# Newton chain of the later blocks in steps 12 to 23 of a fused attention and rational feed-forward kernel

## The chip, the cores and the metric

The kernel runs on one core of a Trainium2 chip. The metric is the device time of one launch in microseconds. A core has five engines with queues of their own, each of which runs its instructions in the order in which they were written: TensorE (PE: matrix products; PEld: its weight loads), VectorE (DVE), ScalarE (ACT), GpSimd (POOL) and SyncE (SP, which issues nearly all transfers here). TensorE writes to the accumulation memory PSUM; VectorE and ScalarE reach both memories, GpSimd only SBUF.

## The reference

Attention inside chunks of 64 positions, then a feed-forward layer with a rational function between its two products:

```python
scores = scale * np.matmul(q_c, k_c.transpose(0, 1, 2, 4, 3))
attn = np.exp(scores - np.max(scores, axis=-1, keepdims=True))
attn = attn / (np.sum(attn, axis=-1, keepdims=True) + 1e-09)
x = np.matmul(attn, v_c)          # then rearranged to 4608 tokens x 512
h = x @ w_in                      # 512 x 2048
P = a[0] + a[1] * h + a[2] * h**2 + a[3] * h**3
Q = 1.0 + np.abs(b[0]) * np.abs(h) + np.abs(b[1]) * h**2
out = (P / (Q + 1e-6)) @ w_out    # 2048 x 512
```

All is float32. Each operand of the large products is split into a high part in TensorE's rounded format and a low part, and three of the four products of parts are summed.

## The kernel before

The tokens are cut into 18 blocks of 256, and the 2048 hidden columns into four stages, so that there are 72 steps. For blocks 0 and 1 the stages alternate; from step 8 on step g is stage g mod 4 of block g div 4. The order of all instructions is written out by hand.

A step has a first product `ff1` (F and f, 48 matrix instructions) into a PSUM tile `ph` of four 128 x 256 pieces; a chain of elementwise instructions, which turns `ph` into g = P/Q split into `ghi` and `glo`; and a second product `ff2` (Z, z and y, 48 instructions, Z and z with `ghi`, y with `glo`) into `po`, two steps later (`LAG`). There are two `ph` buffers, for even and odd steps, and two each of the SBUF tiles A, B, C, `ghi` and `glo`.

Three stretches follow one another:

- The first stage, the string `START`, loads and splits the weights and runs steps 0 to 11 up to their chains.
- The loop over g from `FIRST` = 12 to `CHANGE` = 24, blocks 3 to 5, with the old chain. On ScalarE: Abs and Square of `ph` into A and B, a2 + a3 h into C (a, b, c; lines 351, 355, 359), Ln of Q (line 367) and Exp of its negative (line 371). On VectorE: Q (line 363), the two Horner steps of P (lines 375, 379), `ghi` = P/Q (line 384), and two instructions for the rounding remainder (lines 388, 392). On GpSimd: `glo` (line 397). Around the chain stand the attention of the next blocks: maximum and scale of the scores (M, U), Exp (E, in blocks 4 to 7 sixteen small instructions), sum and scaling (n, N) in stage 0, transposes and their copy (T, K) behind stage 1, the product with V into `psx`, whose tile is the `ph` buffer of the next step, and its split (X on ScalarE, Y on VectorE) in stage 2, together with the scores `pss` of the block after.
- The string `STEADY`, blocks 6 to 17, with the Newton chain (lines 449 to 489): U = |h|, C = na2 + na3 h, V = (U + c0) U, Ln of V, Exp of its negative written over `ph`, two Horner steps of P (p, p2), and t, A2, g, which refine the reciprocal once and multiply. In these blocks the second product uses sums of weights and sums of parts of g (`fast`).

The sums of weights that the later blocks need are made in the loop on GpSimd, one set of four per stage of the second weight: `sums_of` yields groups of instructions, parted by None. In a step with (g - 12) mod 3 of 0 or 1, `make_sums` issues four additions (lines 554 to 566) ahead of the step; in the third, two copies to `hh` on ScalarE (lines 582, 583) and four subtractions in place in `tt` on GpSimd (line 570) are issued, and SP stores `hh` and `tt` in DRAM (lines 574, 575). There is one `tt`, so that the next set begins when its transfer has been read. `newton_coefficients`, called behind step 20, fills the small tile `co`.

```python
for g in range(FIRST, CHANGE):
    ...
    if (g - FIRST) % 3 < 2:
        make_sums()
    one("F f a b", g)
```

Of the kernel before, what the change touches and what calls it, by code (L numbers as in the profile page):

```python
# [10 lines left out]
F32 = mybir.dt.float32  # L11
F32R = mybir.dt.float32r
I32 = mybir.dt.int32
AF = mybir.ActivationFunctionType
ALU = mybir.AluOpType
# [3 lines left out]
P = 128  # L19
# [10 lines left out]
LAG = 2  # L30
KLN = 32
# [16 lines left out]
)  # L48
FIRST = 12
FAST = 6  # L50
CHANGE = NST * FAST
# [14 lines left out]
def tile_chunked_attention_rational_moe(  # L66
# [11 lines left out]
    nc = tc.nc  # L78
    cp = ctx.enter_context(tc.tile_pool(name="cp", bufs=1))
    p2 = ctx.enter_context(tc.tile_pool(name="p2", bufs=2))  # L80
# [13 lines left out]
    ab = cp.tile([P, 8], F32, tag="ab", name="ab")  # L94
    cst = cp.tile([P, 2], F32, tag="cst", name="cst")
    a0, a1, a2, a3 = (ab[:, i:i + 1] for i in range(4))
    b0, b1a = ab[:, 4:5], ab[:, 6:7]
    CQ = 1.0 + 1e-6
    WS = 256.0

    TINY = 2.0 ** -60
# [23 lines left out]
    def load_v(n):  # L125
        if n >= NB:
            return
        v = p2.tile([P, W], F32, tag="vt", name=f"v{n}", bufs=1)
        nc.sync.dma_start(out=v, in_=vP[n])
        loaded["v", n] = v  # L130
# [176 lines left out]
    def att_av(n, u=None, tag="pa"):  # L307
        psx = have("x", n, lambda: bank_pair(tag, f"psx{n}"))

        def cols(g):  # L310
            v, hp = divmod(g, NHP)
            return slice(hp * 128 + v * 64, hp * 128 + v * 64 + 64)

        quarters(cols, psx, loaded["v", n], att["at", n], u)
# [110 lines left out]
                )  # L425
        before[0] = "ff2"

    def newton_coefficients(co):
        na0, na1, na2, na3, c0, kq, lsc, ebias, ib, b1m, nib = (co[:, i:i + 1] for i in range(11))
        ts = nc.vector.tensor_scalar  # L430
        ts(b1m, b1a, TINY, None, ALU.max)
        nc.vector.reciprocal(ib, b1m)
        nc.scalar.activation(ebias, b1m, AF.Ln)
        nc.scalar.activation(c0, b0, AF.Abs, scale=ib)
        ts(nib, ib, -1.0, None, ALU.mult)
        ts(kq, ib, CQ, None, ALU.mult)
        ts(lsc, b1m, 2.0 ** -KLN, None, ALU.mult)
        ts(co[:, 0:4], ab[:, 0:4], nib, None, ALU.mult)
        ts(ebias, ebias, -KLN * math.log(2.0), None, ALU.add)

    total = NB * NST

# [109 lines left out]
    def sums_of(s, tt, hh):  # L552
        def whole(dst, k, half):
            nc.gpsimd.tensor_add(dst, w_part(0, k, s, half).bitcast(F32), w_part(1, k, s, half).bitcast(F32))

        T = [tt[:, i] for i in range(4)]
        yield None
        yield lambda: whole(T[1], 0, 0)
        yield lambda: whole(T[3], 0, 1)
        yield lambda: nc.gpsimd.tensor_sub(T[1], T[3], T[1])  # L560
        yield lambda: whole(T[2], 1, 1)
        yield None
        yield lambda: nc.gpsimd.tensor_add(T[3], T[2], T[3])
        yield lambda: nc.gpsimd.tensor_add(T[2], T[2], T[1])
        yield lambda: whole(T[0], 1, 0)
        yield lambda: nc.gpsimd.tensor_sub(T[0], T[0], T[2])
        yield None

        def low(i):
            nc.gpsimd.tensor_sub(tt[:, i], tt[:, i], hh[:, i].bitcast(F32))  # L570

        def send():
            scratch[s] = dr.tile([P, 2, 4, 512], F32, tag=f"t{s}", name=f"t{s}")
            nc.sync.dma_start(out=scratch[s][:, 0], in_=hh.bitcast(F32))
            nc.sync.dma_start(out=scratch[s][:, 1], in_=tt)
            if s >= 2:
                scratch["b", s] = dr.tile([P, 2, 2, 256], F32, tag=f"b{s}", name=f"b{s}")
                rows = slice(FPS * s, FPS * s + 3, 2)
                for h in range(2):
                    nc.sync.dma_start(out=scratch["b", s][:, h], in_=wo.bitcast(F32)[:, h, rows, 256:512])  # L580

        yield lambda: nc.scalar.copy(hh[:, 1:4:2], tt[:, 1:4:2])
        yield lambda: nc.scalar.copy(hh[:, 0:3:2], tt[:, 0:3:2])
        for i in (1, 3, 2):
            yield lambda i=i: low(i)
        yield lambda: (low(0), send())
# [148 lines left out]
    def ph_tag(g):  # L735
        return "p1" if g == 1 or (g >= 10 and g % 2 == 0) else "p0"
# [18 lines left out]
    def qk(n, u=None):  # L755
# [4 lines left out]

    of_step = lambda f: lambda g: f(*steps[g])
    do = {
        "k": consts, "B": coefficients, "q": qk, "v": load_v, "w": w_load,
        "o": w_low, "s": w_scale, "j": w_join, "i": w_sign, "e": w_sign_dve, "h": w_hi, "hd": w_hi_dve,
        "d": lambda j: w_diff(nc.vector, j), "dp": lambda j: w_diff(nc.gpsimd, j), "r": w_rest, "l": w_lo,
        "S": att_s, "M": att_max, "U": att_sub, "E": att_exp, "n": att_rs, "N": att_norm,
# [14 lines left out]
    def run(program, then=""):  # L781
        words_ = [re.fullmatch(r"([A-Za-z]+)([0-9.]+)(?::(\w+))?", item).groups() for item in program.split()]
        letters = [name for name, _, _ in words_] + [then]
        for k, (name, args, tag) in enumerate(words_):
            ahead[0] = next((x for x in letters[k + 1:] if x in ("F", "f", "Z", "z", "y", "r")), "")
            do[name](*map(int, args.split(".")), **({"tag": tag} if tag else {}))
# [1 line left out]
    run(START, "F")  # L788


    co = p2.tile([P, 32], F32, tag="co", name="co", bufs=1)
    na0, na1, na2, na3, c0, kq, lsc, ebias, ib, b1m, nib = (co[:, i:i + 1] for i in range(11))
    tt = p2.tile([P, 4, 512], F32, tag="raw", name="tt", bufs=3)
    hh = p2.tile([P, 4, 512], F32R, tag="raw", name="hh", bufs=3)
    qk = p2.tile([P, 2, W], F32, tag="raw", name="qk", bufs=3)
    making = [f for s in range(NST) for f in sums_of(s, tt, hh)][1:]

    chain = {
        "U": new_u, "C": new_c, "V": new_v, "p": new_p, "p2": new_p2, "Ln": new_ln, "Ex": new_exp, "t": new_t,
        "A2": new_inv, "g": new_g, "hR": new_hr, "lR": new_lr, "s1": new_s1, "s2": new_s2, "s4": new_s4,  # L800
        "hS": new_hs, "lS": new_ls,
    }
# [84 lines left out]
    def make_sums():  # L887
        while making:
            f = making.pop(0)
            if f is None:  # L890
                break
            f()
# [4 lines left out]
            nc.sync.dma_start(out=qk[:, i, :], in_=src[n])  # L897

    one = lambda names, k: run(" ".join(f"{x}{k}" for x in names.split()))
    for g in range(FIRST, CHANGE):  # L900
        n, stage = steps[g]
        m, early = n + 1, n + 2
        if (g - FIRST) % 3 < 2:
            make_sums()
        one("F f a b", g)
        if stage == 0:
            one("n N", m)
        one("c Q", g)
        if stage == 3:
            one("M U", early)  # L910
        if stage == 2:
            att_av(m, tag=ph_tag(g + 1))
            load_v(m + 1)
            one("S", early)
            load_scores(early + 1)
            one("X", m)
        one("I p", g)
        if stage == 2:
            one("Y", m)
        one("J P", g)  # L920
        if stage == 3:
            one("E", early)
        sums = making[:6] if (g - FIRST) % 3 == 2 else []
        for f in sums[:2]:
            f()
        one("g H R Gp", g)
        for f in sums[2:]:
            f()
        del making[:len(sums) and 7]
        if g == CHANGE - 4:  # L930
            newton_coefficients(co)
        back = steps[g - LAG]
        run(" ".join(f"{x}{g - LAG}" for x in "Zzy"), "F")
        fetch_behind(*back)
        if back[1] == NST - 1:
            store(back[0])
        if stage == 1:
            one("T K", m)

    items = [re.fullmatch(r"(\w+?)(?:_(\d))?([+-]\d+)?", item).groups() for item in STEADY.split()]  # L940
    for b in range(FAST, NB + 1):
        order = list(items)
        if b == NB - 1:
            tail_load()
            order.remove(("hR", "2", None))
            order.insert(order.index(("C", "3", None)) + 1, ("hR", "2", None))
        for op, stage, shift in order:
            n = b + int(shift or 0)
            if n >= NB:
                continue  # L950
            if stage is not None:
                g = NST * n + int(stage)
                if g >= (CHANGE - LAG if op[0] == "Z" else CHANGE):
                    step_op(op, g)
            elif op in ("P1", "o1", "o2", "o3", "o4"):
                if NB - 1 > n >= FAST:
                    fast_out(n, ("P1", "o1", "o2", "o3", "o4").index(op))
                elif op == "P1" and n == FAST - 1:
                    store(n)
            elif n > FAST + (op in ("S", "M", "U", "E")):  # L960
                attention[op](n)
# [36 lines left out]
```

## Time and profile before

| | us |
|---|---|
| median of three runs | 890.44 |
| lowest and highest | 886.53, 891.39 |
| the profiled execution | 888.72 |
| its span, first to last instruction | 886.9 |
| TensorE busy in the span | 847.7 |
| VectorE, ScalarE, GpSimd busy | 770.1, 567.6, 532.4 |
| mean granted TensorE clock | 0.992 |

The profile is one execution, taken by the hardware profiler. Busy times count each engine's instructions; an engine's idle time has a releaser, the instruction that the next one waited for. The granted clock is given as a share of TensorE's full speed. Lines named L384 and so on are those of the kernel before.

### The profile page before, as it was taken

To read this page: it belongs to the slowest core of one execution; us is meant where nothing else is said; L and a number is where in the kernel's file an instruction comes from. 1 tells how busy PE (TensorE), PEld (TensorE's weight loads), DVE (VectorE), ACT (ScalarE), POOL (GpSimd) and SP (SyncE) were. 2 spreads that over 40 slices of the span, in tenths; PEclk is the share of its full clock that TensorE was granted. 3 is DMA by queue.
4 is the path that set the end of the run, shared out by engine and by line. 5 is a ranking of instruction groups with operands and counts; after the bars stand their busy time and mean duration, and the time that the engine had idled before them with its cause. 6 is when DMAs were issued, how large, how long until landed. Compare 5 with 4: busy or idle time off the path is not lost.

```text
span 886.9 us, 21207 instructions
## 1 busy us (share of the span) xinstructions
PE 847.7 (96%) x9108; PEld 831.8 (94%) x9108; DVE 770.1 (87%) x662; ACT 567.6 (64%) x693; POOL 532.4 (60%) x320
## 2 busy tenths in 40 slices
PE   2799999998989899999999999999999999999997
PEld 1689999998989899999999999999999999999996
DVE  6799999879899987888888898889888988887785
ACT  4799986556765556666666666666666666666552
POOL 0114310146687787777868686868686767776771
PEclk9799999999999999999999999999999999999999
DMA  7544250303114155576768677777777777775861
GB/s 290 185 167 167 96 190 14 109 2 126 66 50 143 60 180 175 186 248 198 242 218 256 217 248 229 239 236 237 238 238 232 238 232 238 226 232 172 283 209 36
DMA packets 125469, 162.85 MB, mean 184 GB/s; under 512 B 6848, under 2 KB 111296, under 8 KB 122304
## 3 DMA queue, kind: packets, MB, share of 16 engines
q1 hardware_dynamic: 125216, 161.25, 55.7%
q8 instruction: 71, 1.16, 0.5%
q10 hardware_dynamic: 160, 0.26, 0.1%
q14 instruction: 22, 0.18, 0.1%
HBM read 142.61 MB, written 18.87 MB: 182 GB/s over the span
## 4 chain that ended last, share of the span: by engine, by line
PE 80%; DVE 9%; ACT 5%; DMA 4%; issue 2%; POOL 0%; DVEq 0%; ACTq 0%
PE ph L347 39%; PE acc L606 14%; PE acd L606 11%; PE po L423 10%; PE psx L219 2%; DMA raw<-in_w_in 2%; DMA wo<-t 2%; PE pss L219 2%; DVE B L363 2%; PE pst L299 2%; DVE ghi L384 1%; DVE B L388 1%; DVE C L379 1%; DVE C L375 1%; PE pl L198 1%
## 5 line engine op out<-in xcount | busy, mean ns | idle before, releaser
L347 PE MATMUL ph<-xhi,wi_hi 128*128 128x256 f32 x1152 | 322.4, 280 | 3.2 <-DVE xlo L330 1.6
L347 PE MATMUL ph<-xlo,wi_hi 128*128 128x256 f32 x1152 | 321.1, 279 | 0.1
L347 PE MATMUL ph<-xhi,wi_lo 128*128 128x256 f32 x1152 | 320.9, 279 | 0.0
L347 PEld LDWEIGHTS ph<-xhi,wi_hi 128*128 128x128 f32 x1152 | 218.4, 190 | 4.7 <-DVE xlo L330 1.8
L347 PEld LDWEIGHTS ph<-xlo,wi_hi 128*128 128x128 f32 x1152 | 217.5, 189 | 0.5 <-DVE xlo L330 0.4
L347 PEld LDWEIGHTS ph<-xhi,wi_lo 128*128 128x128 f32 x1152 | 217.5, 189 | 0.0
L541 POOL TENSOR_TENSOR slo<-B,shi 128x1024 fp32r<-128x1024 f32 x46 | 110.7, 2406 | 69.1 <-ACT shi L533 66.9
L451 ACT ACTIVATE U<-ph 128x1024 f32<-128x1024 f32 x48 | 49.5, 1031 | 142.4 <-PE ph L347 142.4
L397 POOL TENSOR_TENSOR glo<-B,A 128x1024 fp32r<-128x1024 f32 x16 | 49.0, 3065 | 97.7 <-DVE B L392 64.4
L460 DVE SCALAR_TENSOR_TENSOR U<-U,co 128x1024 f32<-128x1024 f32 x48 | 84.2, 1754 | 21.7 <-ACT U L451 21.0
L517 POOL TENSOR_TENSOR B<-C 128x512 f32<-128x512 f32 x46 | 69.7, 1515 | 54.6 <-DVE C L489 49.1
L423 PE MATMUL po<-wo,ghi 128*128 128x256 f32 (+2 forms) x768 | 93.6, 278 | 0.0
L481 DVE SCALAR_TENSOR_TENSOR U<-U,co,ph 128x1024 f32<-128x1024 f32 x48 | 60.5, 1259 | 37.6 <-ACT ph L477 37.6
L423 PEld LDWEIGHTS po<-wo,ghi 128*128 128x128 f32 x768 | 90.2, 188 | 0.3
L509 POOL TENSOR_TENSOR graw<-C,graw 128x768 fp32r<-128x768 f32 x46 | 85.4, 1857 | 0.7 <-ACT graw L504 0.7
L606 PE MATMUL acc<-wo,graw 128*128 128x256 f32 x552 | 79.5, 279 | 0.0
L606 PEld LDWEIGHTS acc<-wo,graw 128*128 128x128 f32 x552 | 70.1, 188 | 0.7
L473 ACT ACTIVATE B<-U,cst,co 128x1024 f32<-128x1024 f32 x48 | 59.8, 1246 | 16.4 <-DVE U L460 16.1
L522 POOL TENSOR_TENSOR B<-C,B 128x256 f32<-128x256 f32 x46 | 64.5, 1402 | 3.6
L489 DVE SCALAR_TENSOR_TENSOR C<-C,co,ph 128x1024 f32<-128x1024 f32 x48 | 61.5, 1281 | 1.7
L468 DVE SCALAR_TENSOR_TENSOR C<-C,co,ph 128x1024 f32<-128x1024 f32 x48 | 61.4, 1278 | 1.3
L477 ACT ACTIVATE ph<-B,co 128x1024 f32<-128x1024 f32 x48 | 53.8, 1121 | 12.4 <-DVE C L468 12.4
(118 smaller groups left out, 1850.0 us busy)
## 6 DMA issues: line engine op xcount, KB each, us to landing
wo<-t SPq DMA_DIRECT2D x90, 768.0 KB, 6.6
wo<-t SPq DMA_DIRECT2D x98, 256.0 KB, 3.4
out<-o SPq DMA_DIRECT2D x68, 128.0 KB, 6.2
raw<-in_w_in SPq DMA_DIRECT2D x8, 1024.0 KB, 4.9
raw<-in_w_out SPq DMA_DIRECT2D x8, 1024.0 KB, 5.0
v<-in_vP SPq DMA_DIRECT2D x20, 256.0 KB, 7.8
qk<-in_qT SPq DMA_DIRECT2D x36, 128.0 KB, 6.8
qk<-in_kT SPq DMA_DIRECT2D x36, 128.0 KB, 6.4
```

The costliest lines, as they stand in the source:

```text
L347: nc.tensor.matmul(ph[:, fi, :], w[:, cc, f], x[:, cc, :], start=(k == 0), stop=(k == len(mm) - 1))
L423: nc.tensor.matmul(accs[n][i][:, cols], g[:, fi, i * 128:(i + 1) * 128], w[:, FPS * s + fi, cols], start=start, stop=stop,)
L460: nc.vector.scalar_tensor_tensor(U, U, c0, U, ALU.add, ALU.mult)
L468: nc.vector.scalar_tensor_tensor(C, C, na1, h, ALU.add, ALU.mult)
L473: nc.scalar.activation(ch[key][2], ch[key][1], AF.Ln, bias=cst[:, 0:1], scale=lsc)
L481: nc.vector.scalar_tensor_tensor(V, V, kq, h, ALU.add, ALU.mult)
L489: nc.vector.scalar_tensor_tensor(C, C, na0, h, ALU.add, ALU.mult)
L509: nc.gpsimd.tensor_sub(lo, quads(ch[steps[g]][3])[:, :, 1:4, :], hi.bitcast(F32))
L517: nc.gpsimd.tensor_sub(S[:, 0:2], q[:, 0:1].to_broadcast([P, 2, 2, 128]), q[:, 1:3])
L522: nc.gpsimd.tensor_sub(S[:, 2], q[:, :, 1, :], S[:, 1])
L541: nc.gpsimd.tensor_sub(lo, sbuf[g], hi.bitcast(F32))
L606: nc.tensor.matmul(acc[n][pair][:, bank, col:col + 256], stat, mov, start=start, stop=stop)
```

## The change

Steps 12 to 23 take the Newton chain that the later blocks have. In step g the copy to `ghi` and the subtraction for `glo` are those of step g - 1 (`hR`, `lS`), and for step 23 they follow in `STEADY`. The tile `co` is made ahead of `START`, and the coefficients are computed in `START`: maximum and reciprocal on VectorE (D0) behind block 4's maximum, seven small instructions on ScalarE (C0) ahead of block 4's Exp. The copies to `hh`, the subtractions and the stores of a set of sums stand at the end of their step, behind the second product, the block's store and the transposes' copy, and not between the chain's instructions.

```diff
-    "v4 Z9 c10 Gp9 A3:p0 p10 X3 I10 J10 P10 I11 Y3 S4:pa g10 J11 g11 H10 R10 H11 M4 R11 U4 y8 Gp11 G10 E4 y9 "
+    "v4 Z9 c10 Gp9 A3:p0 p10 X3 I10 J10 P10 I11 Y3 S4:pa g10 J11 g11 H10 R10 H11 M4 D0 R11 U4 y8 Gp11 G10 C0 E4 y9 "
...
+    def newton_reciprocal(_):
+        nc.vector.tensor_scalar(b1m, b1a, TINY, None, ALU.max)
         nc.vector.reciprocal(ib, b1m)
-        nc.scalar.activation(ebias, b1m, AF.Ln)
-        nc.scalar.activation(c0, b0, AF.Abs, scale=ib)
-        ts(nib, ib, -1.0, None, ALU.mult)
-        ts(kq, ib, CQ, None, ALU.mult)
-        ts(lsc, b1m, 2.0 ** -KLN, None, ALU.mult)
-        ts(co[:, 0:4], ab[:, 0:4], nib, None, ALU.mult)
-        ts(ebias, ebias, -KLN * math.log(2.0), None, ALU.add)
+
+    def newton_coefficients(_):
+        act = nc.scalar.activation
+        act(c0, b0, AF.Abs, scale=ib)
+        act(nib, ib, AF.Copy, scale=-1.0)
+        act(kq, ib, AF.Copy, scale=CQ)
+        act(lsc, b1m, AF.Copy, scale=2.0 ** -KLN)
+        act(co[:, 0:4], ab[:, 0:4], AF.Copy, scale=nib)
+        act(ebias, b1m, AF.Ln)
+        act(ebias, ebias, AF.Identity, bias=cst[:, 1:2])
...
-        one("F f a b", g)
+        one("F f", g)
+        chain_ops("U C", g)
         if stage == 0:
             one("n N", m)
-        one("c Q", g)
+        if g > FIRST:
+            chain_ops("hR lS", g - 1)
+        chain_ops("V", g)
         if stage == 3:
             one("M U", early)
...
-        one("I p", g)
+        chain_ops("Ln p", g)
         if stage == 2:
             one("Y", m)
-        one("J P", g)
+        chain_ops("p2 Ex", g)
         if stage == 3:
             one("E", early)
-        sums = making[:6] if (g - FIRST) % 3 == 2 else []
-        for f in sums[:2]:
-            f()
-        one("g H R Gp", g)
-        for f in sums[2:]:
-            f()
-        del making[:len(sums) and 7]
-        if g == CHANGE - 4:
-            newton_coefficients(co)
+        chain_ops("t A2 g", g)
         back = steps[g - LAG]
...
         if stage == 1:
             one("T K", m)
+        if (g - FIRST) % 3 == 2:
+            make_sums()
...
-                if g >= (CHANGE - LAG if op[0] == "Z" else CHANGE):
+                if g >= (CHANGE - LAG if op[0] == "Z" else CHANGE - 1 if op == "hR" else CHANGE):
```

## Rows read from the trace of the kernel before

**Rows 1.** The page's first part: busy us, share of the span, instructions.

```profile
PE 847.7 (96%) x9108; PEld 831.8 (94%) x9108; DVE 770.1 (87%) x662; ACT 567.6 (64%) x693; POOL 532.4 (60%) x320
```

**Rows 2.** Windows: stretch, length, busy us by engine, granted clock, DMA share, GB/s.

```profile
186.00:345.00 159.00, 149.48 (x1620) 148.29 (x1620) 142.69 (x104) 104.18 (x211) 117.96 (x61) 0.99 0.26 94
...
309.30:313.00 3.70, 3.38 (x128) 3.35 (x128) 3.63 (x4) 3.70 (x5) 0.00 (x0) 0.54 0.86 332
```

**Rows 3.** Timeline of TensorE: start, duration, instruction, idle time before it.

```profile
199.73 1.04 PE L299 MATMUL pst<-ident,e 128*128 128x128 f32 x8
200.53 0.37 PE L347 MATMUL ph<-xhi,wi_hi 128*128 128x256 f32 x1
...
208.16 0.45 PE L219 MATMUL psx<-at,v 64*64 64x64 f32 x14 [1.94 <-ACT at L303]
...
210.19 0.40 PE L423 MATMUL po<-wo,ghi 128*128 128x280 f32 x1
217.53 0.39 PE L347 MATMUL ph<-xhi,wi_hi 128*128 128x256 f32 x1 [1.61 <-DVE xlo L330]
...
259.15 0.46 PE L219 MATMUL psx<-at,v 64*64 64x64 f32 x16 [2.26 <-ACT at L303]
...
309.62 0.49 PE L219 MATMUL psx<-at,v 64*64 64x64 f32 x7 [3.60 <-ACT at L303]
...
318.81 0.29 PE L347 MATMUL ph<-xhi,wi_hi 128*128 128x256 f32 x1
```

**Rows 4.** Groups by line, the old chain: busy us, mean ns, idle before.

```profile
L397 POOL TENSOR_TENSOR glo<-B,A 128x1024 fp32r<-128x1024 f32 x16 | 49.0, 3065 | 97.7 <-DVE B L392 64.4 <-DVE sm L263 17.3 <-PE ph L347 7.9
...
L384 DVE SCALAR_TENSOR_TENSOR ghi<-C,ab,A 128x1024 fp32r<-128x1024 f32 x24 | 40.5, 1688 | 1.9 <-ACT A L371 0.3
...
L388 DVE SCALAR_TENSOR_TENSOR B<-B,ghi 128x1024 f32<-128x1024 f32 x24 | 36.4, 1517 | 0.5
```

**Rows 5.** The same groups, of the Newton chain in the later blocks.

```profile
L541 POOL TENSOR_TENSOR slo<-B,shi 128x1024 fp32r<-128x1024 f32 x46 | 110.7, 2406 | 69.1 <-ACT shi L533 66.9 <-DMA wo<-t 1.3
...
L460 DVE SCALAR_TENSOR_TENSOR U<-U,co 128x1024 f32<-128x1024 f32 x48 | 84.2, 1754 | 21.7 <-ACT U L451 21.0
...
L489 DVE SCALAR_TENSOR_TENSOR C<-C,co,ph 128x1024 f32<-128x1024 f32 x48 | 61.5, 1281 | 1.7
...
L464 DVE TENSOR_TENSOR C<-C,ph 128x1024 f32<-128x1024 f32 x48 | 58.1, 1211 | 0.1
...
L477 ACT ACTIVATE ph<-B,co 128x1024 f32<-128x1024 f32 x48 | 53.8, 1121 | 12.4 <-DVE C L468 12.4
...
L499 ACT CAST ghi<-C 128x1024 fp32r<-128x1024 f32 x2 | 2.1, 1044 | 4.0 <-DVE C L489 4.0
```

**Rows 6.** Timelines of VectorE (scaling of block 4; coefficients) and the chain's Exp.

```profile
191.96 2.08 DVE L290 TENSOR_TENSOR e<-e,sm 128x1024 f32<-128x1024 f32 x1
...
300.97 2.10 DVE L438 TENSOR_SCALAR co<-ab,co 128x4 f32<-128x4 f32 x1
...
186.06 4.85 ACT e L274 x32
```

**Rows 7.** Timeline of GpSimd, sums of weights.

```profile
225.21 6.04 POOL L570 TENSOR_TENSOR tt<-tt,hh 128x512 f32<-128x512 f32 x4
237.50 3.99 POOL L554 TENSOR_TENSOR tt<-wo 128x512 f32<-128x512 f32 x2 [6.25 <-DMA t<-tt]
...
265.02 7.01 POOL L570 TENSOR_TENSOR tt<-tt,hh 128x512 f32<-128x512 f32 x4
276.48 2.56 POOL L554 TENSOR_TENSOR tt<-wo 128x512 f32<-128x512 f32 x2 [4.45 <-DMA t<-tt]
...
313.31 2.96 POOL L554 TENSOR_TENSOR tt<-wo 128x512 f32<-128x512 f32 x2 [4.32 <-DMA t<-tt]
```

**Rows 8.** The chain that ended last: start, us, a second and a first product.

```profile
324.45 5.44 PE po L423 x48
329.89 5.48 PE ph L347 x48
```

More of the change, by code (lines that the diff above doesn't have):

```diff
@@ L426, in ff2 @@
         before[0] = "ff2"
[L428 to L431, printed above, removed]
+    co = p2.tile([P, 32], F32, tag="co", name="co", bufs=1)
+    na0, na1, na2, na3, c0, kq, lsc, ebias, ib, b1m, nib = (co[:, i:i + 1] for i in range(11))
+    def newton_reciprocal(_):
+        nc.vector.tensor_scalar(b1m, b1a, TINY, None, ALU.max)
         nc.vector.reciprocal(ib, b1m)
-        nc.scalar.activation(ebias, b1m, AF.Ln)
-        nc.scalar.activation(c0, b0, AF.Abs, scale=ib)
-        ts(nib, ib, -1.0, None, ALU.mult)
-        ts(kq, ib, CQ, None, ALU.mult)
-        ts(lsc, b1m, 2.0 ** -KLN, None, ALU.mult)
-        ts(co[:, 0:4], ab[:, 0:4], nib, None, ALU.mult)
-        ts(ebias, ebias, -KLN * math.log(2.0), None, ALU.add)
+    def newton_coefficients(_):
[7 more added lines that the diff above has]
+        act(ebias, ebias, AF.Identity, bias=cst[:, 1:2])
     total = NB * NST
@@ L762, in tile_chunked_attention_rational_moe @@
     do = {
-        "k": consts, "B": coefficients, "q": qk, "v": load_v, "w": w_load,
+        "k": consts, "B": coefficients, "C": newton_coefficients, "D": newton_reciprocal, "q": qk, "v": load_v, "w": w_load,
         "o": w_low, "s": w_scale, "j": w_join, "i": w_sign, "e": w_sign_dve, "h": w_hi, "hd": w_hi_dve,
@@ L788, in tile_chunked_attention_rational_moe @@
     run(START, "F")
-    co = p2.tile([P, 32], F32, tag="co", name="co", bufs=1)
-    na0, na1, na2, na3, c0, kq, lsc, ebias, ib, b1m, nib = (co[:, i:i + 1] for i in range(11))
     tt = p2.tile([P, 4, 512], F32, tag="raw", name="tt", bufs=3)
@@ L899, in tile_chunked_attention_rational_moe, with chain_ops @@
     one = lambda names, k: run(" ".join(f"{x}{k}" for x in names.split()))
+    def chain_ops(names, g):
+        for name in names.split():
+            chain[name](g)
     for g in range(FIRST, CHANGE):
```

## The prediction

> **What bounds the kernel now.** Read first the busy line of the page [rows 1]: TensorE has 847.7 us of the 886.9 us span, so time is lost only where its queue stops. Steps 12 to 23 lie between about 186 and 345 us; over that window TensorE is busy 149.48 of 159.00 us, VectorE 142.69 and GpSimd 117.96 [rows 2]. The TensorE rows with idle time before them name the stops: 1.94 us before psx in step 14, 1.61 before the first product of step 15, 2.26 before psx in step 18, 3.60 before psx in step 22 [rows 3]: 9.4 us, against 9.52 from the window. Behind the 3.60 us stop the clock drops: 0.54 granted over 3.70 us [rows 2], between the 1.2 and the 2.4 GHz level, which is 0.46 x 3.70 = 1.7 us of lost work. So 9.5 + 1.7 = 11.2 us is all that a change of these steps can give back.
>
> **The change, by engine load.** Both chains have five ScalarE and six VectorE instructions a step and one on GpSimd. Four of the old VectorE instructions read two SBUF tiles and average 1.52 to 1.69 us; in the new chain only V does (1.75), and the five others read PSUM and take 1.21 to 1.28 [rows 4, 5]. With 1.21 and 1.28 for its two PSUM ones the old six make about 8.8 us, the new six 8.0: 0.8 a step. GpSimd's instruction goes from 3.07 to 2.41 us [rows 4, 5]. The coefficients leave step 20, where seven small VectorE instructions, one of them 2.10 us, stood in front of step 21's chain [rows 6]: at least 2.1 us of VectorE. In the first stage they cost two short VectorE instructions ahead of block 4's scales and seven on ScalarE ahead of its 4.85 us row of Exp at 186.06, which waits for those scales [rows 6]. I let that row slip 0.35 us, two short instructions' worth (bounds 0 and 1.0, the second if ScalarE's seven lie on the path too).
>
> Those 2-SBUF instructions and GpSimd exclude each other in the trace: GpSimd's four subtractions take 6.04 us in step 14 and 7.01 in step 17, and V averages 1.75 us where the same operation with a PSUM operand takes 1.28 [rows 5, 7]. The Trainium skill says the same ("SBUF — State Buffer", Who interferes with whom): a VectorE instruction with two SBUF inputs contends with a GpSimd one that reads SBUF, one with at most one SBUF input does not. By that rule alone, three of four collisions would go and the kernel would get the whole 11.2 us; that is the first rival below. I don't follow it, because queue order decides here.
>
> **What the new order makes later.** (1) The old chain frees the ph buffer after its third VectorE instruction, the new one after its sixth, and that sixth lies behind a round trip to ScalarE (Exp waits for p2, t waits for Exp). Steps in a row cost V 1.2 + p 1.25 + p2 1.2 + Exp 1.15 + t 1.3 + A2 1.25 + g 1.3 = 8.65 us on an idle machine. (2) ghi and glo of step g are made in step g+1: the copy hR behind U and C, the subtraction lS on GpSimd behind the four sum instructions that stand at the head of that step's program. C of step g+2 takes the buffer that lS frees. (3) The copies hh, and with them the low parts and their transfer, come at the step's end, on ScalarE behind store and transposes' copy, on GpSimd behind lS of the step before.
>
> **The walk,** with those prices, 1.3 us for a sum instruction, 1.5 for a low one, 2.4 for lS, 5.48 for a first and 5.45 for a second product [rows 5 to 8], 1.1 more for a collision.
> Step 12: block 4's scaling ends on VectorE at 194.0 [rows 6]; V waits out a sum instruction, ready 196.4; p, p2 198.8; Exp 199.95; t, A2, g 203.9. The first product of step 14 needs that buffer and was due at 200.53 [rows 3]: **a new stop of 3.4 us**. Step 13: V 205.1, p2 207.5, Exp 208.7, g 212.6. psx takes ph of step 13 and would be due at 203.9 + 5.48 = 209.4: **stop of 3.2 us**, in place of 1.94. The second product begins at 212.6 + 2.0 for psx and pss (208.16 to 210.19 [rows 3]) = 214.7 and covers xlo (216.1), so step 15's first product starts at 220.1, not 217.53 [rows 3]: 2.6 us late.
> Steps 15 to 18: four first products, three second ones and 0.8 us of transposes later, at 259.15, psx of step 18 is due; its copy is ready at 256.9 and g of step 17 at 258.9, so there is no stop. The old psx started at 259.15 as well [rows 3]: even. The 2.26 us stop is what pays for the early ones.
> Step 17's sums: hh behind the copy, from 256.8; lows 257.9 to 265.0 (four and a collision); step 18's sum instructions wait for tt to land. The trace has 6.25, 4.45 and 4.32 us of waiting for that [rows 7]; I take 4.4 and keep 6.2 for the range. So 269.4, four instructions and a collision 275.7, lS of step 17 278.1. The last part of its second product is due at 259.15 + 2.0 + 5.45 + 5.48 + 3.63 = 275.7: **stop of 2.4 us**.
> C of step 19 waits for the same lS: 278.2, ready 279.4; p, p2 281.9; Exp 283.1; the block's row of Exp, some 4.7, holds ScalarE to 287.8; scaling and V of step 20 290.8; p2 293.2; Exp 294.4; hh 295.4; lows to 302.5; tt 307.0; sums 313.2; lS of step 20 315.6. TensorE, from 278.2: 1.8, then first and second products with transposes to 308.1, psx and pss 310.1, due 313.7: **stop of 1.9 us**. C of step 22, held by that lS, 316.8; hR 317.8; xhi 318.7; xlo 320.0. Step 23's first product is due at 317.5: **stop of 2.5 us**. It starts at 320.0; in the trace of before at 318.81 [rows 3]: **1.2 us late**. Of the old 3.60 us stop and its slow stretch nothing is left, but five stops of 13.4 us stand where four of 9.4 stood.
> Step 24 starts its chain some 4.5 us later on ScalarE, because Exp of step 23 and the row of Exp follow p2; its g is ready at 352.0, due 353.7; lS of step 23 is 0.2 us late. Send and fetches follow lows 2.5 us later than now; the fetch of the step before goes ahead of them. I cost this at 0 to 0.5: the cover is step 25, and without it up to 2 us would show.
> Sum: 888.72 us (the profiled execution: span 886.9 and 1.8 around it) + 1.2 = 889.9. The median of the three times is 890.44, 1.7 above the profiled one; on its scale the forecast is **891.6**. The walk leaves out the clock. If the stop pair of 1.9 and 2.5 us, with 1.8 us of work between, brings a slow stretch as the 3.60 did, 1.7 us come on top (893.3); one after the 3.4 us stop in step 14 costs nothing, as psx waits for VectorE anyway. An error of a collision or two, 1.1 each, lies on either side.
>
> **Rivals.** First, VectorE's relief is paid in full: no stop is left, 890.44 - 11.2 = 879.2. For it: VectorE at 142.69 of 159.00 us. Against: the walk's stops come from serial latency and GpSimd's order. 4%.
> Second, the sum loop is quicker than I walk it: if the tt wait plus collisions shrink by 2.4 us or more a period, lS comes in time and the last three stops (6.8 us) go: 891.6 - 6.8 = 884.8. Against: no wait for tt below 4.32 us shows, and the copies now come later in their step. 11%.
> Third, slower: the loop is longer. If tt takes the 6.25 us of its first landing in steps 18 and 21 as well (it now shares the queue with the stored block and the next loads), lS of 17 and of 20 come 1.8 us later each, and the second carries both: 3.6 us, and the stops pass 3.6 us, so the 1.7 us slow stretch comes with them: 891.6 + 5.3 = 896.9. It decides from about 5.5 us a landing. 21%.
> Fourth, the change does what it says and its stops cost as before: my forecast, between 887 and 895 with a collision more or less and the slow stretch, 64%.
>
> **How the numbers follow.** 0.5% is 4.45 us, about what a measurement of this kernel can tell from no change. Faster by more: rival one and most of rival two, 0.14. Slower by more: rival three and the upper edge of the forecast, 0.24. Same 0.62. The range keeps the forecast's edges and reaches to most of rivals two and three: 886.0 to 896.5.
>
> **What would show it.** Right: TensorE stops before the first product of step 14 (released by VectorE's g) and before psx of step 14, none before psx of step 18, one in the middle of step 19's second product released by GpSimd's lS, two around step 22; C of steps 19 and 22 idle on ScalarE behind lS. The VectorE instructions that read PSUM stay at 1.2 to 1.3 us. Wrong: no stop at lS, or psx of step 22 on time with nothing after it (rival two); stops after step 24, or a wait for fetched sums in steps 26 to 27, would add to the time.

## The result and the profile after

The changed kernel takes 895.21 us (median of twelve runs, 890.55 to 897.94), the kernel before 887.97 us in the twelve runs beside them. The ratio of the means is 1.0072, 95% interval 1.0046 to 1.0098: slower by about 6.4 us. The profiled execution has a span of 892.0 us against 886.9, 5.1 more. Runs in which the chip was disturbed are left out of the ratios, here and below.

The first part of the page after (columns as in [rows 1]):

```profile
PE 854.1 (96%) x9108; PEld 838.5 (94%) x9108; DVE 743.1 (83%) x657; ACT 567.4 (64%) x698; POOL 515.3 (58%) x320
```

VectorE is busy 27.0 us less than in [rows 1], GpSimd 17.1 less, TensorE 6.4 more. TensorE has the same 9108 instructions, so these take longer. The windows after (columns as in [rows 2]) show steps 12 to 23 and, inside them, the two places where the clock falls from 1.00 to 0.50, its 1.2 GHz level:

```profile
186.00:345.00 159.00, 150.56 (x1585) 148.89 (x1585) 113.76 (x94) 99.33 (x202) 94.45 (x58) 0.98 0.27 92
...
208.00:212.00 4.00, 1.39 (x12) 1.18 (x11) 3.69 (x3) 4.00 (x5) 0.00 (x0) 1.00 0.41 89
212.20:215.50 3.30, 3.30 (x124) 3.30 (x128) 2.44 (x3) 2.23 (x3) 2.25 (x1) 0.50 0.31 71
317.00:321.30 4.30, 2.11 (x18) 1.91 (x17) 3.51 (x3) 3.12 (x4) 4.14 (x5) 1.00 0.51 159
321.50:324.70 3.20, 3.20 (x17) 3.20 (x16) 1.99 (x2) 1.12 (x1) 1.97 (x1) 0.50 0.03 11
```

In the 159 us, VectorE gave up 28.9 us and GpSimd 23.5 [rows 2]; TensorE gained 1.1 of busy time, less than it lost to its own slower instructions. The TensorE timeline after, with the stops (columns as in [rows 3]):

```profile
203.49 0.36 PE L347 MATMUL ph<-xhi,wi_hi 128*128 128x256 f32 x1 [3.04 <-DVE C L493]
...
212.20 1.99 PE L219 MATMUL psx<-at,v 64*64 64x64 f32 x64 [2.81 <-ACT C L460]
213.93 1.87 PE L219 MATMUL pss<-qk 64*64 64x64 f32 x64
...
221.49 0.29 PE L347 MATMUL ph<-xhi,wi_hi 128*128 128x256 f32 x1
...
320.29 0.39 PE L347 MATMUL ph<-xhi,wi_hi 128*128 128x256 f32 x1 [2.19 <-DVE xlo L330]
...
333.05 0.29 PE L347 MATMUL ph<-xhi,wi_hi 128*128 128x256 f32 x1
```

Three stops of 8.0 us stand where four of 9.4 stood [rows 3]. Step 23's first product starts at 320.29 (before 318.81), step 24's at 333.05 (329.73): it loses another 1.8 us in one step, in which the clock is low. By step 26 it is 4.1 us late (356.84 against 352.73), at the end 5.1. Step 12 starts 0.8 us earlier in this profile than in the one before (176.73 against 177.50; it is at 175.0 to 180.2 in the profiles of all kernels here). Counted from there the loss is 2.3 us to step 23 and 5.9 to the end.

The chain of waits after, from step 20 to step 24 (start, us, what), shows what holds step 23:

```profile
296.14 0.98 ACT hh L586
...
298.44 4.81 POOL tt L574 x3
303.27 3.95 DMA t<-tt
...
307.36 2.58 POOL tt L558 x2
310.01 1.28 POOL tt L564
311.30 2.24 POOL tt L558
313.54 2.36 POOL glo L548
315.93 1.21 ACT C L460
317.14 0.93 ACT ghi L503
318.07 0.92 ACT xhi L326
319.01 1.24 DVE xlo L330
...
320.29 7.46 PE ph L347 x48
327.75 5.47 PE po L423 x48
```

The copies, the subtractions, the transfer, four sum instructions, lS (`glo`), C, hR (`ghi`), xhi, xlo: link by link the walk of the prediction. The line before the last is the surprise: a first product of 7.46 us. From its first start to its last end, as this one is counted behind a wait, step 24's takes 5.83. (A product that follows another without a wait is counted from the end of the one before and reads 0.16 us less, as the 5.48 in [rows 8] and the 5.67 below.)

### The profile page after: what moved, and what is told of

Same layout as the page of the kernel before. It is cut to its first block, busy times and chain, and to the rows that moved or that the text cites. A ratio compares the mean times of both kernels' runs of the same rounds, so it can differ in the third digit from the quotient of the medians.

```text
span 892.0 us, 21184 instructions
## 1 busy us (share of the span) xinstructions
PE 854.1 (96%) x9108; PEld 838.5 (94%) x9108; DVE 743.1 (83%) x657; ACT 567.4 (64%) x698; POOL 515.3 (58%) x320
## 4 chain that ended last, share of the span: by engine, by line
PE 80%; DVE 8%; ACT 6%; DMA 2%; issue 2%; POOL 2%; SPq 0%; ACTq 0%; DVEq 0%; POOLq 0%
PE ph L347 39%; PE acc L610 14%; PE acd L610 11%; PE po L423 9%; PE psx L219 2%; PE pss L219 2%; ACT e L274 2%; PE pst L299 2%; DVE C L472 1%; DVE U L464 1%; DMA wo<-t 1%; DVE C L468 1%; DVE sm L255 1%; DMA Bqk<-in_kT 1%; POOL tt L574 1%
## 5 line engine op out<-in xcount | busy, mean ns | idle before, releaser
L455 ACT ACTIVATE U<-ph 128x1024 f32<-128x1024 f32 x60 | 62.0, 1033 | 167.2 <-PE ph L347 167.2
L464 DVE SCALAR_TENSOR_TENSOR U<-U,co 128x1024 f32<-128x1024 f32 x60 | 101.1, 1685 | 41.2 <-ACT U L455 40.1
L485 DVE SCALAR_TENSOR_TENSOR U<-U,co,ph 128x1024 f32<-128x1024 f32 x60 | 75.8, 1263 | 50.1 <-ACT ph L481 50.1
L477 ACT ACTIVATE B<-U,cst,co 128x1024 f32<-128x1024 f32 x60 | 74.7, 1245 | 20.9 <-DVE U L464 20.4
L481 ACT ACTIVATE ph<-B,co 128x1024 f32<-128x1024 f32 x60 | 67.2, 1120 | 32.0 <-DVE C L472 31.9
L460 ACT ACTIVATE C<-ph,co 128x1024 f32<-128x1024 f32 x60 | 72.6, 1211 | 9.7 <-POOL glo L548 9.7
L493 DVE SCALAR_TENSOR_TENSOR C<-C,co,ph 128x1024 f32<-128x1024 f32 x60 | 76.8, 1280 | 2.1
L472 DVE SCALAR_TENSOR_TENSOR C<-C,co,ph 128x1024 f32<-128x1024 f32 x60 | 76.6, 1277 | 1.6
L468 DVE TENSOR_TENSOR C<-C,ph 128x1024 f32<-128x1024 f32 x60 | 72.6, 1210 | 4.8 <-ACT C L460 4.8
L489 DVE SCALAR_TENSOR_TENSOR ph<-U,ph 128x1024 f32<-128x1024 f32 x60 | 73.6, 1227 | 1.7
```

Source lines behind the costliest of these rows:

```text
L464: nc.vector.scalar_tensor_tensor(U, U, c0, U, ALU.add, ALU.mult)
L468: nc.vector.tensor_mul(C, C, h)
L472: nc.vector.scalar_tensor_tensor(C, C, na1, h, ALU.add, ALU.mult)
L477: nc.scalar.activation(ch[key][2], ch[key][1], AF.Ln, bias=cst[:, 0:1], scale=lsc)
L485: nc.vector.scalar_tensor_tensor(V, V, kq, h, ALU.add, ALU.mult)
L489: nc.vector.scalar_tensor_tensor(h, V, 2.0, h, ALU.subtract, ALU.mult)
```

## The experiments

Each stands against the kernel before in runs of its own on the same chip. "The change" is the kernel after. Two experiments are compared by these ratios, and a difference of two ratios is known to some 0.25 to 0.35% on either side.

**e1: hR and lS ahead of the sum instructions.**

```diff
-        if (g - FIRST) % 3 < 2:
-            make_sums()
         one("F f", g)
...
             chain_ops("hR lS", g - 1)
+        if (g - FIRST) % 3 < 2:
+            make_sums()
```

> The changed kernel with the copy hR and the subtraction lS of the step before issued ahead of the four sum instructions of a step, not behind them. Queue order (my theory: C of step g+2 waits on GpSimd for lS, which stands behind sums that wait for a transfer): the idle time of 2.2 us before the first product of step 23 and the slow stretch of about 1.8 us behind it go, the stop of C of step 22 on ScalarE (5.2 us) too; 4 us below the changed kernel, ratio to the kernel before about 1.003. Round trip (rival: the chain through ScalarE and the longer hold of ph is what costs): nothing in steps 15 to 23 depends on the sums, ratio stays at 1.007. Product rate (second rival: the 48 matrix instructions of a first product follow one another every 118 ns in most steps of the changed kernel and every 114 ns in most of the one before): rate and time stay, ratio 1.007.

889.45 us, ratio 1.0012 (0.9993 to 1.0031), some 5.3 us better than the change. TensorE's waits between 186 and 345 us (us in all, times, longest):

```profile
PE ph L347 <- DVE C L493: 3.1, 1, 3.1
PE psx L219 <- ACT C L460: 2.8, 1, 2.8
PE po L423 <- DVE glo L397: 0.2, 1, 0.2
```

The stop at step 23 is gone, and with it the slow product (it starts at 317.45 and takes 5.83 us from first start to last end). The two stops in step 14 stand. So the stop at step 23 comes from GpSimd's order.

**e2: the old chain in steps 12 and 13, the Newton chain from step 14 on.**

```diff
+NEWTON = 14
...
-        chain_ops("U C", g)
+        if g < NEWTON:
+            one("a b", g)
+        else:
+            chain_ops("U C", g)
...
```

> The changed kernel with the old chain in steps 12 and 13 and the Newton chain from step 14. Round trip: the 3.0 us stop before the first product of step 14 goes, the one before psx of step 14 shrinks from 2.8 us (with its slow stretch) to the 1.9 us of the kernel before; step 15 starts about 4 us earlier and keeps it, since psx of step 18 had no stop; ratio about 1.003. Queue order: the two early stops go as well, but the sums' loop only shifts with them, and the stop before step 23 stays at about 2 us. If the early stops were paid back by slack later (the stop of step 18 in the kernel before was), nothing is gained: 1.007. Product rate: 118 ns stay, ratio 1.005 to 1.007.

891.0 us, 1.0034 (1.0017 to 1.0051): 3.4 us better than the change. The stops released by `C` of lines 493 and 460 go; 1.6 and 0.9 us before two psx, 1.5 behind `glo` and 3.3 in front of two first products stay, and step 23's first product takes 7.46 us again. So the stops in step 14 come from the Newton chain in steps 12 and 13.

**e3: e1 and e2 together.**

```diff
+NEWTON = 14
...
+        if (g - FIRST) % 3 < 2:
+            make_sums()
+        if g < NEWTON:
+            one("c Q", g)
...
```

> Both edits: old chain in steps 12 and 13, and lS ahead of the sums. If stops are the whole cost, 4 + 4 us go: ratio about 0.998, TensorE idle between 186 and 345 us about 3.5 us. If the product rate carries half of the cost (12 steps x 48 x 4 ns = 2.3 us in the loop alone), the stops go and the ratio stays at or above 1.000.

885.58 us, 0.997 (0.9955 to 0.9986): 9.1 us better than the change, about the sum of the two, and better than the kernel before. TensorE is busy 155.25 of the 159 us, with two stops of 1.6 us. Both causes are real, and within the intervals their costs add up.

**e4: the kernel before with the coefficients in the first stage only.**

```diff
-... H10 R10 H11 M4 R11 U4 y8 Gp11 G10 E4 y9 "
+... H10 R10 H11 M4 D0 R11 U4 y8 Gp11 G10 C0 E4 y9 "
...
-        if g == CHANGE - 4:
-            newton_coefficients(co)
```

> The kernel before with one part of the change: the tile and the coefficients in the first stage, nothing behind step 20; old chain in steps 12 to 23. Stops: VectorE has 2.7 us less in front of step 21's chain, so that the 3.6 us stop before psx of step 22 becomes about 1.5 us and the slow stretch behind it goes; 0.35 us lost in step 12: 3 to 4 us faster than before, ratio 0.996. If the coefficients in the first stage are what the change loses by: ratio above 1.002. Product rate: if it hangs on where the small tile lies (it is the first of its pool here, as in the changed kernel), the first products run at 118 ns here as well and 2 to 5 us are lost: ratio about 1.000 in sum.

893.69 us, 1.0054 (1.003 to 1.0078), where 0.996 was expected: the part that removes 2.1 us of VectorE work makes the old kernel slower. Two causes came into question: what the freed VectorE meets, and the tile `co`, which now is the first of its pool. The next four runs part them.

**e5: the kernel before with `co` placed first in its pool and nothing else.** The instructions are the same; all other tiles of the pool lie 128 bytes higher.

```diff
+    co = p2.tile([P, 32], F32, tag="co", name="co", bufs=1)
+
     total = NB * NST
...
-    co = p2.tile([P, 32], F32, tag="co", name="co", bufs=1)
```

> The kernel before, with one thing changed: the small tile co (128 bytes a partition) is made ahead of the first stage, as in the changed kernel, so that all tiles behind it lie 128 bytes higher; every instruction is the same. Placement theory: the first products of steps 12 to 23 run at 118 ns a matrix instruction and not 114, the slow ones more than double over the run, 4 us slower, ratio about 1.004 to 1.006. Rival (the 118 ns come with the other instructions, or with the execution): rate and time as before, ratio 1.000 within 0.002.

890.86 us, 1.0031 (1.0009 to 1.0052). Four first products in its chain of waits (start, us, what):

```profile
280.02 5.67 PE ph L347 x48
...
343.65 5.67 PE ph L347 x48
...
367.46 5.44 PE ph L347 x48
379.13 5.65 PE ph L347 x48
```

Nearly every first product takes either 5.44 to 5.48 us or 5.65 to 5.67, that is 114 or 118 ns for each of its 48 matrix instructions. In the kernel before, steps 12 to 25 run at the faster rate (one is in [rows 8]) and later about three in four; here steps 12 to 25 run at the slower one and later about every second. Start to start, the mean over steps 12 to 71 is 114.8 ns before and 116.4 here (products at a low clock left out, here and below). Placement alone costs 0.3%, with an interval of 0.1 to 0.5: less than the theory's 0.4 to 0.6, more than its rival's 0.2.

**e6: the change with `co` made where it is first used,** so that the other tiles lie as before.

```diff
-    co = p2.tile([P, 32], F32, tag="co", name="co", bufs=1)
...
     def newton_reciprocal(_):
...
+        co = p2.tile([P, 32], F32, tag="co", name="co", bufs=1)
```

> The changed kernel with the tile co made at its first use, behind the other tiles, which then lie where they lie in the kernel before; the order of all instructions is that of the change. Placement theory: first products at 114 ns, the stops stay as they were; 4 us faster than the changed kernel, ratio to before about 1.002. Stops alone (my forecast's theory): ratio stays at 1.007.

890.14 us, 1.0032 (1.0012 to 1.0052): 0.4% better than the change; the mean of its first products is back at 114.9 ns. The stop behind lS of step 17 that the prediction named, and the change did not show, is there:

```profile
280.06 0.50 PE L423 MATMUL po<-wo,glo 128*128 128x256 f32 x2 [1.44 <-POOL glo L550]
```

TensorE came there 0.1 us sooner than in the change (278.62 against 278.74); the rest is lS, which ended at 280.01 and not 278.68. It took 3.35 us, in the change 2.39, while V beside it took 1.69 and not 3.55: the two met the other way round. The slow stretch in step 14 (0.50 from 213.4 to 216.6 us) stays; at step 23 there is a stop of 1.26 us and no slow stretch.

**e7: e3 with `co` made late.**

```diff
+NEWTON = 14
...
     def newton_reciprocal(_):
...
+        co = p2.tile([P, 32], F32, tag="co", name="co", bufs=1)
...
+        if (g - FIRST) % 3 < 2:
+            make_sums()
+        if g < NEWTON:
+            one("c Q", g)
```

> Old chain in steps 12 and 13, lS ahead of the sums, and the tile co at its first use. If stops and placement add, 4 us below the same kernel with the early tile (0.997): ratio about 0.992, near 881 us. If placement has no part: 0.997.

883.15 us, 0.9943 (0.9922 to 0.9964): faster than both kernels, if less than the 0.992 expected. Its window from 186 to 345 us (columns as in [rows 2]):

```profile
186.00:345.00 159.00, 155.18 (x1669) 154.05 (x1668) 126.26 (x100) 105.50 (x203) 105.31 (x63) 1.00 0.32 110
```

And all that TensorE waited for by more than 1 us in it:

```profile
PE ph L348 <- DVE xlo L331: 1.4, 1, 1.4
PE psx L220 <- ACT at L304: 1.3, 1, 1.3
```

**e8: e4 with `co` made late.**

```diff
     def newton_reciprocal(_):
...
+        co = p2.tile([P, 32], F32, tag="co", name="co", bufs=1)
```

> The kernel before with the coefficients in the first stage and the tile co at its first use: one part of the change without the shift. Placement theory: 114 ns again, and the 1.005 of the same kernel with the early tile falls to 1.000 or below; the gain by stops (a shorter stop before psx of step 22) shows as 0.997 to 1.000. If the coefficients' new place is what loses (two new stops late in the loop stood in the trace of that kernel): ratio stays above 1.003.

894.35 us, 1.0057 (1.003 to 1.0084): no better than e4 although the mean of its first products is back at 115.2 ns. So here placement isn't the cause. GpSimd around step 21, in the kernel before:

```profile
303.01 5.98 POOL L570 TENSOR_TENSOR tt<-tt,hh 128x512 f32<-128x512 f32 x4
...
319.85 3.38 POOL L397 TENSOR_TENSOR glo<-B,A 128x1024 fp32r<-128x1024 f32 x1
```

And in e8, with VectorE, ScalarE and TensorE of the same stretch:

```profile
304.14 7.97 POOL L576 TENSOR_TENSOR tt<-tt,hh 128x512 f32<-128x512 f32 x4
...
306.55 2.19 DVE L388 SCALAR_TENSOR_TENSOR B<-B,ghi 128x1024 f32<-128x1024 f32 x1
308.77 2.20 DVE L392 SCALAR_TENSOR_TENSOR B<-C,ab,B 128x1024 f32<-128x1024 f32 x1
...
324.18 2.36 POOL L397 TENSOR_TENSOR glo<-B,A 128x1024 fp32r<-128x1024 f32 x1
...
326.58 1.12 ACT L351 ACTIVATE A<-ph,ab 128x1024 f32<-128x1024 f32 x1 [11.01 <-POOL glo L397]
...
326.60 2.15 PE L423 MATMUL po<-wo,glo 128*128 128x256 f32 x16 [1.38 <-POOL glo L397]
```

The coefficients had held VectorE back while GpSimd subtracted. Without them, step 21's two remainder instructions, which read two SBUF tiles, fall into the subtractions: both sides slow down (2.19 us where 1.23 is usual, 7.97 where 5.98 was), the transfer lands later, the sums start at 316.23 and not 313.31 [rows 7], and `glo` of step 21, queued behind four of them, ends 3.3 us later, although step 12 starts 2.5 us earlier in e8's profile. ScalarE's Abs for step 23 and TensorE wait for it; at the end of that chain the transposes of step 25 stop for 3.80 us.

**e9: the kernel before with the sums behind `glo` of their step.**

```diff
-        if (g - FIRST) % 3 < 2:
-            make_sums()
         one("F f a b", g)
...
         del making[:len(sums) and 7]
+        if (g - FIRST) % 3 < 2:
+            make_sums()
```

> The kernel before with one edit: the four sum instructions of a step stand behind that step's glo on GpSimd, not ahead of the step. Theory: in the old chain GpSimd's order costs TensorE nothing as long as the coefficients hold VectorE back in step 20, because glo of step 21 (319.85 in the kernel before) is done before TensorE needs it. The four stops (1.94, 1.61, 2.26, 3.60 us) stay within a collision or two: 885 to 890 us. Rival: the sums at the head of a step are what makes VectorE's two-SBUF instructions slow in front of psx; then the stops before psx shrink by some 3 us in all and the time is 884 or less.

890.05 us, 1.0022 (0.9997 to 1.0048). The time is at the theory's upper edge, its reason isn't the theory's: the stop before psx of step 14 goes and the one of step 22 shrinks to 0.8 us, but the one before psx of step 18 grows to 8.9 us, as in the next run.

**e10: e8 with the sums behind `glo`** (the edit against e8).

```diff
-        if (g - FIRST) % 3 < 2:
-            make_sums()
         one("F f a b", g)
...
+        if (g - FIRST) % 3 < 2:
+            make_sums()
         back = steps[g - LAG]
```

> The coefficients in the first stage (tile co made late), and the sums of a step behind its glo on GpSimd; else the kernel before. Theory: with the coefficients alone (894.4 us) the freed VectorE ran into GpSimd's four subtractions (7.97 us in place of 5.98), the transfer and the sums came 2.9 us later, and glo of step 21 stood behind them; with glo ahead of the sums the stop of 1.4 us in step 21's second product goes and step 23 starts its chain some 3 us earlier, so that most of the 3.8 us stop before the transposes of step 25 goes too: 887 to 890 us. Rival: the loss with the coefficients alone comes from something else (ScalarE's seven instructions in the first stage, or where instructions lie): the time stays at 893 to 895.

889.49 us, 1.0025 (1.0006 to 1.0044), 0.3% better than e8, about as much as its interval, as the theory has it: no stop behind `glo` and none after step 23 is left. But the sums now end too late for the copies `hh`, which hold ScalarE and the transposes' copy behind it (ScalarE, then TensorE, in e10):

```profile
258.97 1.04 ACT L589 CAST hh<-tt 128x1024 fp32r<-128x1024 f32 x1 [5.56 <-POOL tt L572]
...
261.89 1.98 PE L219 MATMUL psx<-at,v 64*64 64x64 f32 x64 [8.94 <-ACT at L303]
```

**e11: the kernel before with copies, subtractions and stores at the end of their step.**

```diff
-        sums = making[:6] if (g - FIRST) % 3 == 2 else []
...
         if stage == 1:
             one("T K", m)
+        if (g - FIRST) % 3 == 2:
+            make_sums()
```

> The kernel before with the copies to hh, the subtractions and the stores at the end of their step and nothing else. Theory: the copies leave the front of ScalarE's queue ahead of step 13's and 16's next chain, but the subtractions start 2 to 3 us later and collide with other VectorE instructions; no stop depends on them but that before psx of step 22: 886 to 891 us, no change that counts. Rival: the later copies push the tt transfer and with it the sums in front of glo: 892 or more.

890.48 us, 1.0034 (1.0014 to 1.0054), inside the theory's span of 886 to 891 but not its "no change". The stops are 8.6 us, less than before. Its steps 15 to 22 run at 118 ns a matrix instruction though no tile has moved; why is open.

**e12: e7 without the Newton chain** (e10 and e11 together; the edit against e8).

```diff
-        if (g - FIRST) % 3 < 2:
-            make_sums()
         one("F f a b", g)
...
+        if (g - FIRST) % 3 < 2:
+            make_sums()
         back = steps[g - LAG]
...
         if stage == 1:
             one("T K", m)
+        if (g - FIRST) % 3 == 2:
+            make_sums()
```

> All of the best version but the Newton chain: coefficients in the first stage, tile co made late, sums behind glo, copies at the step's end, old chain in steps 12 to 23. Theory: the Newton chain's instructions that read PSUM, which GpSimd does not slow, bring a part of the gain themselves, so that this kernel stands 3 to 6 us above the 883.15 of the best version: 886 to 889. Rival: the gain is all queue order and the chain is worth nothing: 882 to 885.

887.02 us, 0.9982 (0.9961 to 1.0004): 0.4% slower than e7, so the Newton chain is worth 3 to 4 us, as expected; not for the reason expected. In e12 the copy waits for the sums again, and the first product of step 19 stops (ScalarE and TensorE of e12), at a clock of 0.50 from 266 to 270 us:

```profile
260.39 1.05 ACT L589 CAST hh<-tt 128x1024 fp32r<-128x1024 f32 x1 [5.13 <-POOL tt L572]
...
267.34 0.58 PE L347 MATMUL ph<-xhi,wi_hi 128*128 128x256 f32 x1 [5.02 <-DVE xlo L330]
```

In e7 the same copy runs at 254.48 and waits for nothing:

```profile
254.48 1.06 ACT L590 CAST hh<-tt 128x1024 fp32r<-128x1024 f32 x1
```

The old chain makes `glo` at the end of its own step, so sums behind it end in the next (in e12 the `glo` ahead of that copy starts at 249.10 us, and the sums behind it end at 260.36); the Newton chain's `glo` is that of the step before and is ready early, so the sums can stand behind it and still be in time (239.36 and 247.04 in e7). TensorE is busy 1.75 us less than in e7 in the 159 us (153.43), and the slow product, at 159 ns a matrix instruction, costs 1.9. Together that is about what the two ratios put between them (0.39%, 3.5 us); the two profiles lie 5.8 us apart, so some of that is open. What the PSUM operands bring by themselves wasn't parted from it, and another order of the sums around the old chain, which might avoid the late copy, wasn't tried.

## Why the prediction was right or wrong

The forecast was 891.6 us, 1.2 more than before on the scale of its three runs; measured, the change costs 0.72%, 6.4 us. The range to 896.5 held the time with luck: the three runs before stood 2.5 us above the twelve (890.44 against 887.97), and 6.4 us on top of the three would be 896.8. A time within 0.5% was called likeliest (0.62), and slower, given 0.24, came. Step by step:

- **The first stage, priced too high.** The slip of 0.35 us for block 4's row of Exp didn't come: it starts 8.5 us behind step 12's first product (185.25), before 8.6 (186.06 [rows 6]).
- **Step 14, right.** The first product was forecast at 203.9 and started at 203.49, behind VectorE's g; psx at 212.6, and it started at 212.20. e2 shows the cause.
- **Step 14's slow stretch, wrong.** The text said that a slow stretch after the 3.4 us stop costs nothing. The clock fell not there but at psx, behind the second stop (granted 0.50 from 212.2 to 215.5 us): psx and pss took 3.5 us, not 2.0, and step 15 began at 221.49, not 220.1.
- **Steps 15 to 18, a term missing.** Each first product was priced at 5.48 us [rows 8] and took 5.67: 0.8 us over four. With the 1.4 us from step 15 that is 2.2 of the 2.5 us by which psx of step 18 is late (261.69, forecast 259.15). That it has no stop was right.
- **lS of steps 17 and 20: the times right, the stops not.** lS of step 17 was forecast done at 278.1 and ended at 278.68; lS of step 20 at 315.6 and 315.89. For step 17 that is in part luck: the subtractions began at 260.02, not 257.9, and the transfer took 5.07 us, not 4.4, but of the two collisions of 1.1 us that were priced in none shows (6.01 for four subtractions, 5.2 for four sums). TensorE came 2 to 3 us later than in the walk (278.74 for the part with `glo`, forecast 275.7), and so the stops of 2.4 and 1.9 us shrank to nothing and 0.1: time lost ahead of a stop is taken off the stop. In e6, where TensorE came at the same time, one collision of lS with V is most of the 1.44 us. C of step 19 did wait for lS, 2.53 us, as forecast; that TensorE has no stop behind lS is one of the signs that the prediction named for being wrong.
- **Step 23, right.** C of step 22 waited 5.24 us for lS and ran at 315.93; xlo was ready at 320.25 (forecast 320.0), the first product started at 320.29: 1.5 us late, forecast 1.2 (2.3 late counted from the start of step 12). e1 shows the cause.
- **The slow stretch at step 23, left out of the sum.** It was named, with 1.7 us, as what may come on top. It came: 7.46 us where step 24's takes 5.83, 1.6 us. The stop before it was 2.19 us, shorter than the 2.26 in step 18 before [rows 3], which had brought none (granted 1.00 from 257 to 265 us).
- **Steps 24 and 25, a little over.** They were costed at 0 to 0.5; TensorE loses 0.8, of which 0.4 is a stop before the transposes and 0.4 two slower products.
- **Placement, not seen at all.** "The tile `co` is made ahead of the first stage" stood in the change's description and had no term. It costs 0.3 to 0.4% by three pairs (e5 against before 0.31, the change against e6 0.40, e3 against e7 0.27) and nothing by the fourth (e4 against e8, -0.03), each with an interval of some 0.2 to 0.4 to either side. In the change's 0.40 may also lie the slow stretch at step 23, which e6's profile hasn't. The change without placement, e6, lies 2.8 us above before; the forecast's 1.2 with 1.7 for one slow stretch is 2.9, but that fit is partly luck: e6 has its slow stretch in step 14, where it was priced at nothing, and two of the walk's five stops are there at about half their size (1.44 and 1.26 for 2.4 and 2.5 us), one not at all. So what the sum lacked is this term and the slow stretches; the walk found four of its five waits in e6, but not the size of each.
- **Part by part.** The coefficients' move was costed at a slip of 0.35 us and a gain of 2.1 us of VectorE; by itself it costs 0.55% (e4, e8), since the freed engine walks into GpSimd. In the changed kernel that collision can't take the same form, as V alone of its six VectorE instructions reads two SBUF tiles; what the move costs there wasn't measured.

The first rival, VectorE's relief paid in full, fell clearly: VectorE gave up 28.9 us in these steps and TensorE gained 1.1. The instructions behaved as priced; groups of the change between 186 and 345 us (columns as in [rows 4]):

```profile
L548 POOL TENSOR_TENSOR glo<-C,ghi 128x1024 fp32r<-128x1024 f32 x11 | 27.4, 2492 | 30.2 <-ACT ghi L503 30.2
...
L464 DVE SCALAR_TENSOR_TENSOR U<-U,co 128x1024 f32<-128x1024 f32 x13 | 22.4, 1726 | 15.9 <-ACT U L455 15.9
...
L485 DVE SCALAR_TENSOR_TENSOR U<-U,co,ph 128x1024 f32<-128x1024 f32 x12 | 15.4, 1281 | 15.0 <-ACT ph L481 15.0
...
L468 DVE TENSOR_TENSOR C<-C,ph 128x1024 f32<-128x1024 f32 x12 | 14.5, 1212 | 4.8 <-ACT C L460 4.8
```

Those with a PSUM operand take 1.21 to 1.28 us whatever GpSimd does; V swings from 1.27 to 3.55 us (the one at 276.22, beside lS and a sum). That agrees with the Trainium skill ("SBUF — State Buffer", Who interferes with whom), and e8 shows the same as a loss. In the change, whose wait ended last was set by the order in GpSimd's queue (e1) and by the Newton chain in steps 12 and 13 (e2).

The second and third rivals hung on the landing of `tt`, 4.4 us in the walk, less than 2.0 for the quicker loop, 5.5 and more for the longer: the rows show 4.01, 5.07 and 4.11. Neither came; the loss has the third's size by another way.

## What to carry to other kernels

Count for each moved instruction who stands behind it in its queue: here the same chain is 0.7% slower or 0.6% faster, by whether four GpSimd instructions stand ahead of or behind one short one, which chain the first two steps have, and where one small tile lies. An engine that is given time back starts its next work sooner, and that may fall into another engine's accesses: look at what runs in the freed stretch before booking the gain. After a change that adds a tile, compare the duration of an instruction group that was not touched; if it has moved, a part of the result may be placement. Here allocating the tile later took back 0.3 to 0.4% in two kernels and nothing in a third (e4, e8).

## What the hardware showed that was not expected

- Runs of 48 matrix instructions of 256 columns go at 114 or at 118 ns each, a whole product at one rate, at a granted clock of 1.00. The six kernels with all tiles 128 bytes higher have means of 116.3 to 116.5 ns over steps 12 to 71, the eight others 114.7 to 115.4. With e5 the instructions are identical, so placement decides most of it; but without a moved tile e11 has eight products in a row at 118 and e8 five, and what in the placement matters is open.
- One stop does not tell whether a slow stretch follows. 2.19 us before step 23 was followed by a product of 7.46 us (granted 0.50 from 321.5 to 324.7 us), 1.91 us before step 23 of e2 by the same (0.50 from 316.9 to 320.2), and the pair of 3.04 and 2.81 us in step 14 by psx and pss at 1.7 times their time; 2.26 us in step 18 of the kernel before [rows 3] and 1.26 us in step 23 of e6 by none.
- In these stretches the clock is at one of its two levels, 0.50 (1.2 GHz) or 1.00 (2.4 GHz). The 0.54 of [rows 2], which the prediction put between the levels, is a mean over both: the clock was at 0.50 from 309.4 to 312.7 us.
